# Zeros as warming weights, three rows of batch 2 transposed by DMA, and a new order of the instructions around the first two tiles

## The chip, the cores and the metric

The kernel runs on one core of one Trainium2 chip. The metric is the device time of one execution in microseconds (us). The core has five engines with queues of their own: TensorE (PE, with its weight loads shown as PEld), VectorE (DVE), ScalarE (ACT), GpSimd (POOL) and SyncE (SP). Each engine executes its instructions in program order. Transfers are issued from the queues of SP, ACT and POOL.

## The reference

Blockwise causal attention over 8 batches, 8 heads, 576 positions and head size 64, followed by a gated feed-forward layer on the result:

```python
scores = scale * np.matmul(q, k.transpose(0, 1, 3, 2))
mask = block_i >= block_j                      # blocks of 64 positions
scores = np.where(mask, scores, -1000000000.0)
attn = softmax(scores)
attn_out = np.matmul(attn, v)                  # (8, 8, 576, 64)
x = attn_out.transpose(0, 2, 1, 3).reshape(4608, 512)
gate = np.maximum(x @ w_gate, 0.0)             # 512 -> 1536
val = x @ w_val
out = (gate * val) @ w_out                     # 1536 -> 512
```

All inputs and the output are float32; the kernel computes in bfloat16 with float32 sums.

## The kernel before

**Rows.** A row `r = 4*b + hp` is one pair of heads `hp` of batch `b`; there are 32 rows. Each batch has 512 main positions (four blocks of 128) and 64 last positions, which the kernel calls tails. For a row the kernel needs q and k with the head dimension on the partitions (`qTm`, `kTm`, and `qTt`, `kTt` for the tails). Then `scores_all` makes the scores in three pieces, each in a pair of PSUM banks, and `exp` on ACT (L520) turns each piece into `attnT`; the corners of the mask are zeroed by `corners`. `head_av` (L648) multiplies with v (`v_bf`, with a column of ones for the sum) in PSUM banks 6 and 7, and `normalise` (L592 and L593 on DVE) divides and writes `xnat`. Finally `xnat` is transposed into `xT[:, hp, :]` of the batch: by `to_xT_pe` (four transposes on PE, L693, and a fifth, L699, for the 64 last positions from batch 2 on; then a copy out of PSUM by ACT or DVE), or by `to_xT_dma` (two DMA transposes on SP's queue, L707 and L711, with no work for PE). The tile `xnat` has three buffers, `xT` three.

**Feed-forward.** `ffn_gen` is a generator over nine tiles of 512 positions: tile j is batch j's main positions, tile 8 all tails. A tile has twelve groups f: four matmuls with `wg` and four with `wv` (L752), a Relu on ACT (L761), a product on DVE (L766, `hT`); then four outputs of twelve matmuls with `wo` (L782), each copied by DVE (L794, `ob`) and stored. `parts(n)` in the hand-written order emits n steps of four such matmuls, 0.86 us each; `ffn(n)` emits whole groups. They are what PE does while other engines work on the attention.

**PSUM.** `take(n)` gives the least recently taken of the banks 0 to 5 (a pair for `take(2)`). So three pairs serve the scores, the groups of the feed-forward layer and the single banks of outputs, and whoever takes a pair waits until its last user has been copied out. Banks 6 and 7 (`AV`) serve `head_av`, the transposes of batch 1 (`pe_mains`, L423) and the sorting of its v rows (`sort_v`, L373).

**Batches.** Batch 0 and 1 (class `Early`) come through staged float32 loads on SP, casts by POOL, and PE transposes. The first halves of batch 1 (heads 0 to 3: rows 4, 5) and the second (heads 4 to 7: rows 6, 7) are loaded, cast and transposed apart; `sort_v(0)` and `sort_v(4)` order the v rows of each. The tails of batches 0 and 1 are loaded together (`Tails.load`, six DMAs), cast (`cast_qk`, L213; `cast_v`, L220), transposed by eight PE transposes (`tails.pe`, L232) and copied to `qTt` and `kTt` (L240). Batch 2 and 3 are staged and cast too, but transposed by DMA (`e2.transpose`, L396, and `transpose_tails`, L438 and L439) and reordered by copies (`unpermute`, L407). From batch 4 on, POOL issues casting loads (L459), and DMA transposes write `qTm` and `kTm` directly. The stage buffers are ten, taken in turn.

**Order.** Everything is under a manual schedule: the order of the calls is the order on every engine's queue. The start has warming matmuls (`junk`, L831), which write a bank that nothing reads: the weights are `ident`, which POOL makes, the moving operand is `zeros`, which DVE sets. Then batch 0 is computed with no feed-forward work to mix in; from the first `parts(1)` on, tile 0 and then the first half of tile 1 are mixed with batch 1 by a list written out by hand (lines 902 to 1007). The loop over r = 8 to 31 does the rest in a regular way: `head_av(r-1)` around `scores_all(r)`, then the transposes of row r-1, then `ffn`. In the pass r = 8 the loads, casts and DMA transposes of batch 3 are issued; in the pass r = 11 the loads of batch 4 begin.

Of the kernel before, what the change touches and what calls it, by code (L numbers as in the profile page):

```python
# [17 lines left out]
def kernel(  # L18
# [10 lines left out]
    nc = tc.nc  # L29
# [454 lines left out]
    def load_w_half(i, g, which=(0, 1)):  # L484

        sts = []
        for t in which:
            dst, src = ((wg, moe_w_gate), (wv, moe_w_val))[t]
            lo = 512 * i + 256 * g
            st = new_stage(1024).rearrange("p (c n) -> p c n", c=4)  # L490
            nc.sync.dma_start(
                st, src[:, lo : lo + 256].rearrange("(c p) f -> p c f", p=128)
            )
            sts.append((dst[i][:, :, 256 * g : 256 * g + 256], st))
        return sts
# [4 lines left out]
    def cast_w(sts, eng):  # L500
        for dst, st in sts:
            eng(dst, st)  # L502
# [319 lines left out]
    def parts(n):  # L822

        for _ in range(n):
            next(gen)
            part[0] += 4
            done[0] += 4

    def junk(n, bank):
        for _ in range(n):  # L830
            nc.tensor.matmul(  # L831
                bank.rearrange("p (j n) -> p j n", j=4),
                ident,
                zeros[:, None, :].to_broadcast([128, 4, 128]),
                start=True,
                stop=True,
            )
# [4 lines left out]
    with tc.manual_schedule(engines={E.PE, E.DVE, E.Activation, E.Pool, E.SP}):  # L842
# [10 lines left out]
        constants(0, nc.vector)  # L853
        constants_tail(0, nc.vector)
        selection(nc.vector.memset, nc.vector.tensor_copy)
        junk(7, banks[:, 0])
        constants(1, nc.gpsimd)
        constants_tail(1, nc.gpsimd)
        token_order(pool)
# [52 lines left out]
        es = (e0, e1)  # L912
        w_2, w_out = {}, {}
        xt = sb.tile([128, 4, 128], BF, name="xtail")
        w_2[0] = load_w_half(2, 0)
        e1.load_qk(0, 4)
        parts(1)
        w_2[1] = load_w_half(2, 1)
        parts(1)
        cast_w(w_2[0], pool)  # L920
        e1.load_v_packed(0)
        e1.cast_qk(0, 4, (pool, pool))
        cast_w(w_2[1], pool)
        parts(3)
        w_out[0] = load_w_out(0)
        parts(2)
        w_out[1] = load_w_out(1)
        parts(5)
        e1.cast_v_packed(0, pool)
        parts(1)  # L930
        w_out[2] = load_w_out(2)
        parts(3)
        cast_w(w_out[0], pool)
        e1.pe_mains(0, (dve, dve), banks[:, AV : AV + 2])
        cast_w(w_out[1], pool)
        parts(1)
        e1.load_qk(4, 4)
        e1.pe_mains(1, (act, dve), banks[:, AV : AV + 2])
        cast_w(w_out[2], pool)
        scores_all(4, False)  # L940
        parts(3)
        corners(4, nc.vector)
        parts(1)
        e1.cast_qk(4, 4, (pool, pool))
        e1.sort_v(0, (act, dve), banks[:, AV : AV + 2])
        scores_all(5, False)
        heads_av(4)
        parts(1)
        e1.load_v_packed(4)
        corners(5, nc.vector)  # L950
        parts(1)
        heads_av(5)
        parts(1)
        tails.load()
        tails.cast_qk(pool)
        to_xT_pe(4, (act,), None)
        parts(3)
        e1.cast_v_packed(4, pool)
        parts(2)
        e2.load_qk(0, 4)  # L960
        e2.load_qk(4, 4)
        e2.load_v_chunks(0)
        e2.load_v_chunks(1)
        e2.load_tails((0, 1))
        e2.load_tails((2,))
        tails.cast_v(0, pool)
        e1.pe_mains(2, (dve, dve), banks[:, AV : AV + 2])
        parts(1)
        e1.pe_mains(3, (dve, dve), banks[:, AV : AV + 2])
        scores_all(6, False)  # L970
        tails.pe((dve, dve))
        corners(6, nc.vector)
        to_xT_pe(5, (act,), banks[:, AV + 1])
        scores_all(7, False)
        e1.sort_v(4, (dve, dve), banks[:, AV : AV + 2])
        parts(1)
        corners(7, nc.gpsimd)
        tails.cast_v(1, pool)
        parts(2)
        heads_av(6)  # L980
        scores_last(0)
        scores_tails(0, (0,))
        scores_tails(0, (1,))
        e2.cast_qk(0, 4, (pool, pool))
        e2.cast_qk(4, 4, (pool, pool))
        to_xT_pe(6, (act,), None)
        e2.cast_tails((pool, pool))
        heads_av(7)
        parts(1)
        e2.transpose(0)  # L990
        e2.transpose(1)
        parts(1)
        scores_last(1)
        to_xT_pe(7, (dve,), banks[:, AV + 1])
        parts(2)
        tails_av(0, 0)
        tails_av(0, 1)
        tails_of(0, xt)
        scores_tails(1, (0,))
        scores_tails(1, (1,))  # L1000
        parts(1)
        e2.unpermute(0, (dve, pool))
        parts(4)
        e2.unpermute(1, (dve, pool))
        parts(2)
        e2.transpose_tails()
        parts(1)
        for r in range(8, 4 * B):
            b, hp = divmod(r, 4)
            tails_av(1, 0) if r == 8 else head_av(r - 1, 0)  # L1010
            scores_all(r)
            tails_av(1, 1) if r == 8 else head_av(r - 1, 1)
            tails_of(1, xt) if r == 8 else heads_to_xnat(r - 1)
            if r > 12:
                to_xT_dma(r - 1)
            if r < 10:
                e2.unpermute(r - 6, (dve, dve))
            elif 11 <= r < 15:
                e3.unpermute(r - 11, (dve, dve))
            corners(r, nc.vector)  # L1020
            ffn(12 if r < 13 else 8)
            if hp == 0:
                scores_last(b)
            if 8 < r < 13:
                to_xT_pe(r - 1, (act,))
            if r == 8:
                tails_to_xT(xt, dve)
                e2.cast_v_tail(pool)
                e2.cast_v_chunks(0, pool)
                e2.cast_v_chunks(1, pool)  # L1030
                e3 = Early(3)
                e3.load_qk(0, 4)
                e3.load_tails((0, 1))
                e3.load_qk(4, 4)
                e3.load_tails((2,))
                e3.load_v_chunks(0)
                e3.load_v_chunks(1)
                e3.cast_qk(0, 4, (pool, pool))
                e3.cast_tails((pool, pool))
                e3.cast_qk(4, 4, (pool, pool))  # L1040
                e3.transpose(0)
                e3.transpose(1)
                e3.transpose_tails()
            if r == 11:
                for g in range(2):
                    e3.cast_v_chunks(g, pool)
                e3.cast_v_tail(pool)
            if hp == 3 and b + 2 < B:
                load_qkv(b + 2, (0, 1))
            if b >= 3 and b + 1 < B:  # L1050
                if hp == 0:
                    load_qkv(b + 1, (2,))
                if hp == 2:
                    dma_transposes(b + 1)
            ffn(8 if r < 12 else 0 if r == 12 else 28)
# [32 lines left out]
```

## Time and profile before

| what | value |
|---|---|
| median of 3 runs | 368.8 us (368.2 to 370.13) |
| the profiled execution, its own time | 367.89 us |
| its span, first to last instruction | 366.1 us |
| granted TensorE clock, mean | 0.999 |
| DVE, ACT, POOL busy | 46%, 46%, 31% of the span |
| moved by DMA | 51.02 MB, mean 139 GB/s |

The span lies inside the execution's own time; 1.8 us lie around it. A row of a timeline gives start, duration (of all instructions merged in the row), engine, line, operation, output and input, a count, and in brackets the idle time of the engine before it and what ended it. In the chain of waits a row has start, duration and what was on the chain then. In a table by stretches each engine has its busy time in the stretch and a count. The end of a merged PE row includes about 0.17 us in which the next matmuls already run, so PE's steps are read from start to start.

### The profile page before, as it was taken

What the parts mean: (1) busy time and instruction counts of PE and PEld (TensorE: products, weight loads), DVE (VectorE), ACT (ScalarE), POOL (GpSimd) and SP (SyncE); (2) the same over time, 40 slices, a digit from 0 to 9 for tenths busy, and PEclk for the clock granted to TensorE, in tenths of its full rate; (3) what the DMA queues carried; (4) which work ended last, traced back from release to release, by engine and by line L of the source; (5) the groups of instructions that cost most, each with busy time, mean ns of one, the idle gap of its engine ahead of it and who ended that gap; (6) DMA issues with size and microseconds to landing.
All of it is one profiled execution on the core that took longest, in us unless ns stands there. A gap on an engine that the chain in (4) does not pass through costs nothing.

```text
span 366.1 us, 7493 instructions
## 1 busy us (share of the span) xinstructions
PE 355.9 (97%) x2981; PEld 187.3 (51%) x2981; DVE 167.6 (46%) x335; ACT 167.3 (46%) x263; POOL 114.8 (31%) x158
## 2 busy tenths in 40 slices
PE   7899998999999999999999999999999999999995
PEld 3544455555555455555555555555555544444443
DVE  5744455466465543444344443544344424333432
ACT  4933716556756653565346543654264303302310
POOL 7756746275878307700590031000000000000000
PEclk9999999999999999999999999999999999999999
DMA  8999999979999979996899949173200130020013
GB/s 253 288 348 351 379 255 323 158 198 238 194 190 139 141 154 98 165 104 118 104 182 73 148 86 124 28 138 75 75 16 18 47 102 1 3 86 29 2 39 104
DMA packets 139652, 51.02 MB, mean 139 GB/s; under 512 B 117473, under 2 KB 133601, under 8 KB 139617
## 3 DMA queue, kind: packets, MB, share of 16 engines
q1 hardware_dynamic: 77952, 34.29, 41.1%
q0 software_dynamic: 56384, 7.08, 40.7%
q10 hardware_dynamic: 5280, 9.18, 7.1%
q8 instruction: 23, 0.38, 0.4%
q14 instruction: 13, 0.10, 0.1%
HBM read 37.75 MB, written 9.44 MB: 129 GB/s over the span
## 4 chain that ended last, share of the span: by engine, by line
PE 93%; ACT 4%; DVE 1%; issue 0%; POOL 0%; ACTq 0%; DVEq 0%; POOLq 0%
PE banks L752 51%; PE banks L782 25%; PE banks L648 7%; PE banks L514 6%; ACT attnT L520 2%; PE banks L831 1%; PE banks L611 1%; PE banks L693 1%; PE banks L423 1%; ACT wo L520 1%; ACT v_p L520 1%; PE banks L373 1%; DVE kTt L240 0%; DVE ob L794 0%; ACT xT L700 0%
## 5 line engine op out<-in xcount | busy, mean ns | idle before, releaser
L520 ACT ACTIVATE attnT<-banks 128x1024 bf16<-128x1024 f32 (+1 forms) x118 | 84.9, 808 | 59.7 <-PE banks L514 59.4
L761 ACT ACTIVATE gate_sb<-banks 128x512 bf16<-128x512 f32 x108 | 64.9, 603 | 102.4 <-PE banks L752 102.2
L766 DVE TENSOR_TENSOR hT<-gate_sb,banks 128x512 bf16<-128x512 bf16 x108 | 74.1, 687 | 80.5 <-PE banks L752 74.2
L752 PE MATMUL banks<-xT,wg 128*128 128x512 bf16 x384 | 99.6, 379 | 0.6 <-ACT attnT L520 0.4
L752 PE MATMUL banks<-xT,wv 128*128 128x512 bf16 x384 | 99.4, 379 | 0.0
L782 PE MATMUL banks<-wo,hT 128*128 128x512 bf16 (+1 forms) x444 | 97.2, 373 | 0.0
L752 PEld LDWEIGHTS <-wv 128*128 128x128 bf16 x432 | 42.1, 98 | 50.4 <-POOL wv L502 0.3
L782 PEld LDWEIGHTS <-hT 128*128 128x128 bf16 x444 | 42.3, 98 | 46.3 <-issue 0.2
L752 PEld LDWEIGHTS <-wg 128*128 128x128 bf16 x432 | 40.8, 98 | 46.3 <-issue 1.3
L794 DVE COPY ob<-banks 128x512 f32<-128x512 f32 (+1 forms) x37 | 25.1, 677 | 52.4 <-PE banks L782 52.3
L459 POOL DMA_DIRECT2D v_bf<-in_v_dram x16 | 14.3, 908 | 66.9 <-PE banks L648 66.9
L648 PE MATMUL banks<-v_bf,attnT 128*128 128x65 bf16 x792 | 33.4, 194 | 0.6 <-DVE attnT L579 0.3
L648 PEld LDWEIGHTS <-attnT 128*128 128x128 bf16 x792 | 29.1, 98 | 8.6 <-issue 1.0
L514 PE MATMUL banks<-qTm,kTm 64*128 64x512 bf16 (+3 forms) x256 | 25.0, 300 | 2.4 <-ACT attnT L520 1.5
L593 DVE TENSOR_TENSOR xnat<-banks,recip 128x640 bf16<-128x640 f32 (+2 forms) x36 | 25.9, 721 | 1.2
L514 PEld LDWEIGHTS <-kTm 64*128 64x128 bf16 x512 | 17.1, 94 | 10.8 <-issue 1.7
L592 DVE RECIPROCAL recip<-banks 128x10 f32<-128x10 f32 (+3 forms) x38 | 8.0, 210 | 31.2 <-PE banks L648 29.3
L459 POOL DMA_DIRECT2D k_bf<-in_k_dram x16 | 14.2, 928 | 1.7 <-DMA v_bf<-in_v_dram 1.1
L459 POOL DMA_DIRECT2D q_bf<-in_q_dram x16 | 14.4, 935 | 0.5 <-DMA v_bf<-in_v_dram 0.5
L579 DVE MEMSET attnT<- 64x192 uint32 x27 | 5.9, 218 | 18.0 <-ACT attnT L520 17.3
L752 PE MATMUL banks<-xTt,wg 128*128 128x512 bf16 x48 | 12.3, 379 | 0.0
L752 PE MATMUL banks<-xTt,wv 128*128 128x512 bf16 x48 | 12.3, 379 | 0.0
(99 smaller groups left out, 199.9 us busy)
## 6 DMA issues: line engine op xcount, KB each, us to landing
out_dram<-ob ACTq DMA_DIRECT2D x32, 256.0 KB, 2.4
stage<-in_moe_w_gate_dram SPq DMA_DIRECT2D x6, 512.0 KB, 8.7
stage<-in_moe_w_val_dram SPq DMA_DIRECT2D x6, 512.0 KB, 8.8
stage<-in_q_dram SPq DMA_DIRECT2D x6, 512.0 KB, 8.1
stage<-in_k_dram SPq DMA_DIRECT2D x6, 512.0 KB, 8.2
stage<-in_moe_w_out_dram SPq DMA_DIRECT2D x6, 512.0 KB, 9.5
stage<-in_v_dram SPq DMA_DIRECT2D x8, 256.0 KB, 6.7
q_bf<-in_q_dram POOLq DMA_DIRECT2D x16, 128.0 KB, 6.7
```

Source lines behind the costliest of these rows:

```text
L459: nc.gpsimd.dma_start(dst, src[b, :, 128 * c : 128 * c + n, :].rearrange("h p d -> p h d"),)
L514: nc.tensor.matmul(o, kTm[b % 2][ps, c, hp, :], x, start=True, stop=True)
L520: nc.scalar.activation(out, sc, AF.Exp, scale=scale)
L579: eng.memset(three[:, :, :, 0:64], 0.0)
L592: nc.vector.reciprocal(recip, av[:, :, :, 64])
L593: nc.vector.tensor_tensor(out=out, in0=av[:, :, :, 0:64], in1=recip.to_broadcast([rows, heads, n, 64]), op=AX.mult,)
L648: nc.tensor.matmul(av[:, 0, p, :], w, vb[:, c, h, :], start=(p == 0), stop=(c == p), skip_group_check=True,)
L752: nc.tensor.matmul(out[f][:, t, :], (wg, wv)[t][i][:, c, fo : fo + 128], x[:, c, :], start=(c == 0), stop=(c == 3),)
L761: nc.scalar.activation(gate[f], out[f][:, 0, :], AF.Relu)
L766: nc.vector.tensor_tensor(out=h, in0=gate[f], in1=out[f][:, 1, :], op=AX.mult)
L782: nc.tensor.matmul(ops[:, g, 0 : n1 - n0], hT[f][:, 128 * s : 128 * (s + 1)], wo[i][:, f % 4, n0:n1], start=(f == 0), stop=(f == 11),)
L794: nc.vector.tensor_copy(ob, ops[:, g, 0 : n1 - n0])
```

## The change

It has three edits. The warming matmuls take `zeros` as weights too, and the first batch of them is nine instead of seven. In the loop, rows 8, 9 and 10 (of batch 2) go to `xT` by `to_xT_dma` instead of `to_xT_pe`; row 11 stays with PE. The list of calls between the first steps of tile 0 and the loop has a new order: the loads of `w_2` and of batch 1 are written behind five steps; scores of rows 4 and 5 come before the last group of tile 0; the copies of k out of PSUM in the first two `pe_mains` go to ACT; row 5's `head_av` comes after four more output steps; the second half of batch 1 and the tails come later, with `tails.pe` behind the last output of tile 0 and `scores_all(7)` behind `sort_v(4)`; on SP the loads of the tails come before the second half of v, and the v rows of batch 2 before its q and k; on POOL `tails.cast_v(0)` comes before `tails.cast_qk`, and batch 2's casts before `tails.cast_v(1)`. The number of feed-forward steps before the loop is the same.

```diff
@@ junk @@
-                ident,
+                zeros,
                 zeros[:, None, :].to_broadcast([128, 4, 128]),
@@ start @@
-        junk(7, banks[:, 0])
+        junk(9, banks[:, 0])
@@ list @@
+        parts(5)
         w_2[0] = load_w_half(2, 0)
+        cast_w(w_2[0], pool)
         e1.load_qk(0, 4)
-        parts(1)
         w_2[1] = load_w_half(2, 1)
-        parts(1)
-        cast_w(w_2[0], pool)
+        parts(5)
+        e1.cast_qk(0, 4, (pool, pool))
         e1.load_v_packed(0)
-        e1.cast_qk(0, 4, (pool, pool))
+        parts(2)
+        w_out[0] = load_w_out(0)
+        parts(1)
         cast_w(w_2[1], pool)
+        parts(1)
+        w_out[1] = load_w_out(1)
+        parts(2)
+        e1.pe_mains(0, (dve, act), banks[:, AV : AV + 2])
+        e1.cast_v_packed(0, pool)
+        parts(1)
+        w_out[2] = load_w_out(2)
+        scores_all(4, False)
+        e1.pe_mains(1, (dve, act), banks[:, AV : AV + 2])
+        parts(2)
+        corners(4, nc.vector)
+        scores_all(5, False)
+        cast_w(w_out[0], pool)
+        cast_w(w_out[1], pool)
+        e1.load_qk(4, 4)
+        e1.sort_v(0, (act, dve), banks[:, AV : AV + 2])
+        parts(4)
+        cast_w(w_out[2], pool)
+        tails.load()
+        e1.load_v_packed(4)
+        heads_av(4)
+        corners(5, nc.vector)
+        parts(2)
+        e2.load_v_chunks(0)
+        e2.load_v_chunks(1)
         parts(3)
-        w_out[0] = load_w_out(0)
-        parts(2)
-        w_out[1] = load_w_out(1)
-        parts(5)
-        e1.cast_v_packed(0, pool)
-        parts(1)
-        w_out[2] = load_w_out(2)
-        parts(3)
-        cast_w(w_out[0], pool)
-        e1.pe_mains(0, (dve, dve), banks[:, AV : AV + 2])
-        cast_w(w_out[1], pool)
-        parts(1)
-        e1.load_qk(4, 4)
-        e1.pe_mains(1, (act, dve), banks[:, AV : AV + 2])
-        cast_w(w_out[2], pool)
-        scores_all(4, False)
-        parts(3)
-        corners(4, nc.vector)
+        heads_av(5)
         parts(1)
         e1.cast_qk(4, 4, (pool, pool))
-        e1.sort_v(0, (act, dve), banks[:, AV : AV + 2])
-        scores_all(5, False)
-        heads_av(4)
-        parts(1)
-        e1.load_v_packed(4)
-        corners(5, nc.vector)
-        parts(1)
-        heads_av(5)
-        parts(1)
-        tails.load()
-        tails.cast_qk(pool)
-        to_xT_pe(4, (act,), None)
-        parts(3)
-        e1.cast_v_packed(4, pool)
-        parts(2)
+        e1.pe_mains(2, (dve, dve), banks[:, AV : AV + 2])
+        tails.cast_v(0, pool)
+        parts(1)
+        e1.pe_mains(3, (act, dve), banks[:, AV : AV + 2])
+        scores_all(6, False)
+        to_xT_pe(4, (dve,), banks[:, AV])
+        parts(1)
         e2.load_qk(0, 4)
         e2.load_qk(4, 4)
-        e2.load_v_chunks(0)
-        e2.load_v_chunks(1)
+        to_xT_pe(5, (dve,), banks[:, AV])
         e2.load_tails((0, 1))
+        parts(1)
         e2.load_tails((2,))
-        tails.cast_v(0, pool)
-        e1.pe_mains(2, (dve, dve), banks[:, AV : AV + 2])
-        parts(1)
-        e1.pe_mains(3, (dve, dve), banks[:, AV : AV + 2])
-        scores_all(6, False)
-        tails.pe((dve, dve))
-        corners(6, nc.vector)
-        to_xT_pe(5, (act,), banks[:, AV + 1])
+        parts(1)
+        tails.cast_qk(pool)
+        tails.pe((act, dve))
+        e1.cast_v_packed(4, pool)
+        e1.sort_v(4, (dve, dve), banks[:, AV : AV + 2])
+        corners(6, nc.gpsimd)
         scores_all(7, False)
-        e1.sort_v(4, (dve, dve), banks[:, AV : AV + 2])
-        parts(1)
-        corners(7, nc.gpsimd)
-        tails.cast_v(1, pool)
-        parts(2)
         heads_av(6)
-        scores_last(0)
+        e2.cast_qk(0, 4, (pool, pool))
+        e2.cast_qk(4, 4, (pool, pool))
+        e2.cast_tails((pool, pool))
         scores_tails(0, (0,))
         scores_tails(0, (1,))
-        e2.cast_qk(0, 4, (pool, pool))
-        e2.cast_qk(4, 4, (pool, pool))
+        scores_last(0)
         to_xT_pe(6, (act,), None)
-        e2.cast_tails((pool, pool))
+        corners(7, nc.vector)
         heads_av(7)
+        parts(2)
+        to_xT_pe(7, (dve,), banks[:, AV + 1])
         parts(1)
         e2.transpose(0)
         e2.transpose(1)
-        parts(1)
-        scores_last(1)
-        to_xT_pe(7, (dve,), banks[:, AV + 1])
         parts(2)
+        tails.cast_v(1, pool)
+        parts(1)
         tails_av(0, 0)
         tails_av(0, 1)
         tails_of(0, xt)
         scores_tails(1, (0,))
         scores_tails(1, (1,))
         parts(1)
+        scores_last(1)
         e2.unpermute(0, (dve, pool))
-        parts(4)
-        e2.unpermute(1, (dve, pool))
         parts(2)
         e2.transpose_tails()
-        parts(1)
+        e2.unpermute(1, (dve, dve))
+        parts(3)
@@ loop @@
-            if r > 12:
+            if r > 8 and r != 12:
                 to_xT_dma(r - 1)
...
-            if 8 < r < 13:
+            if r == 12:
                 to_xT_pe(r - 1, (act,))
```

More of the change, by code (lines that the diff above doesn't have):

```diff
@@ L914 @@
         xt = sb.tile([128, 4, 128], BF, name="xtail")
+        parts(5)
         w_2[0] = load_w_half(2, 0)
+        cast_w(w_2[0], pool)
         e1.load_qk(0, 4)
+        w_2[1] = load_w_half(2, 1)
+        parts(5)
+        e1.cast_qk(0, 4, (pool, pool))
+        e1.load_v_packed(0)
+        parts(2)
+        w_out[0] = load_w_out(0)
         parts(1)
[L918 removed]
+        cast_w(w_2[1], pool)
         parts(1)
[L920 to L925 removed]
+        w_out[1] = load_w_out(1)
         parts(2)
[L927 to L928 removed]
+        e1.pe_mains(0, (dve, act), banks[:, AV : AV + 2])
         e1.cast_v_packed(0, pool)
```

## The prediction

> **What bounds the kernel now.** I read the page first (span, shares, chain), then the busy times by stretches, then the timelines of PE, ACT, DVE, POOL and SP where PE is not full.
>
> ```profile
> span 366.1 us, 7493 instructions
> ...
> PE 93%; ACT 4%; DVE 1%; issue 0%; POOL 0%; ACTq 0%; DVEq 0%; POOLq 0%
> ```
> ```profile
> 30.00:40.00 10.00, 9.61 (x62) 4.88 (x61) 3.84 (x7) 5.63 (x10) 6.91 (x8) 1.00 1.07 363
> 40.00:50.00 10.00, 9.59 (x99) 5.30 (x98) 4.78 (x12) 4.49 (x8) 7.05 (x8) 1.00 1.08 345
> 50.00:60.00 10.00, 8.49 (x80) 4.97 (x79) 6.70 (x17) 5.37 (x9) 4.05 (x7) 1.00 1.12 292
> 60.00:70.00 10.00, 9.66 (x177) 6.53 (x177) 4.71 (x11) 4.27 (x7) 6.52 (x11) 1.00 0.91 209
> ```
> PE carries 93% of the chain. The columns of the stretches are us, then busy time of PE, PEld, DVE, ACT and POOL, clock, DMA share, GB/s: PE misses 0.4, 0.4, 1.5 and 0.3 us of these 40, and it is here that the list is reordered. So there are three things to win: PE work itself, PE's waits between 36 and 64 us, and the start. The waits:
>
> ```profile
> 37.99 1.02 PE L752 MATMUL banks<-xT,wg 128*128 128x512 bf16 x4 [0.40 <-ACT attnT L520]
> ...
> 46.04 0.78 PE L648 MATMUL banks<-v_bf,attnT 128*128 128x65 bf16 x20 [0.29 <-DVE attnT L579]
> ...
> 55.05 0.87 PE L232 MATMUL banks<-ident,perm 128*128 128x128 bf16 x8 [0.42 <-POOL perm L213]
> 55.76 0.39 PE L693 MATMUL banks<-order,xnat 128*128 128x128 bf16 x4
> 56.46 0.97 PE L514 MATMUL banks<-qTm,kTm 64*128 64x512 bf16 x7 [0.31 <-ACT attnT L520]
> 58.00 0.27 PE L514 MATMUL banks<-qTm,kTm 64*128 64x256 bf16 x1 [0.57 <-DVE kTt L240]
> ...
> 63.47 0.40 PE L693 MATMUL banks<-order,xnat 128*128 128x128 bf16 x4 [0.34 <-DVE xnat L593]
> ```
> A row's end holds some 0.17 us of overlap, so from start to start the waits are a little longer than the brackets: 0.5 before 37.99, 0.45 before 46.04, 0.45 before 55.05, 0.5 before 56.46, 0.9 before 58.00, 0.4 before 63.47; with the small ones (0.1 to 0.25 each) about 3.9 us. No reordering can win more than that.
>
> **Edit 1, the start.**
>
> ```profile
> 0.83 0.11 DVE L108 MEMSET zeros<- 128x64 uint32 x1 [0.83 <-PEq L1072]
> 1.97 3.17 PE L831 MATMUL banks<-zeros,ident 128*128 128x512 bf16 x7 [1.97 <-POOL ident masks.py:199]
> 4.41 0.43 DVE L326 CAST q_bf<-stage 128x512 bf16<-128x512 f32 x1
> ```
> ```profile
> 5.14 0.85 PE banks L423 x8
> ...
> 35.17 0.45 PE banks L423 x8
> 35.62 0.86 PE banks L752 x4
> ```
> ```profile
> 21.76 1.04 POOL L502 CAST wv<-stage 128x1024 bf16<-128x1024 f32 x1 [0.47 <-DMA stage<-in_moe_w_val_dram]
> ...
> 22.92 1.03 PE L752 MATMUL banks<-xT,wv 128*128 128x512 bf16 x4
> ```
> Eight transposes take 0.85 us at 5.14 and 0.45 at 35.17: PE runs at half speed at first, although the clock column reads 1.00. Today the warming waits for POOL's `ident` until 1.97; with zeros alone it waits for DVE only (0.83 + 0.11) and starts near 1.0. Nine matmuls of 3.17/7 = 0.45 end by 5.0, about when the first cast (4.41 + 0.43 = 4.84) lets the transposes begin: no delay, 0.1 at worst. If full speed comes 1 us sooner, the first transposes and scores win up to 0.6 us. But the win ends at 22.92: that step needs `wv`, cast at 21.76 + 1.04 = 22.80 after a wait for DMA, and the loads do not move. So 0.12 us can pass. I take -0.1, with ends of +0.1 and -0.12. The Trainium skill (TensorE: Matmul & The Clock Gate, on the clock gate) says that warm-up is a free-running window of about 3.4 us and not a count of matmuls; by it the two extra matmuls bring nothing, and the earlier start brings between nothing and a whole window, by the window's phase: in the first case this edit is worth 0 and the sum below is 366.7. Half speed still at 5.14, 3.2 us after the first matmul, agrees with a window; the phase no row here shows.
>
> **Edit 2, the order.** Up to 35.17 PE's sequence is unchanged, and the loads and casts that it needs keep their order on SP and POOL. From there I walk through the new list, each engine in the order of its queue, with these durations:
>
> ```profile
> 36.59 0.69 DVE L766 TENSOR_TENSOR hT<-gate_sb,banks 128x512 bf16<-128x512 bf16 x1 [0.40 <-PE banks L752]
> ...
> 56.22 1.73 DVE L240 COPY kTt<-banks 64x256 bf16<-64x256 bf16 x4
> ...
> 59.09 1.29 DVE L382 CAST v_bf<-banks 128x512 bf16<-128x512 f32 x2 [0.86 <-PE banks L373]
> ```
> ```profile
> 36.74 0.58 ACT L435 COPY qTm<-banks 128x512 bf16<-128x512 bf16 x1 [0.94 <-PE banks L423]
> 37.34 2.49 ACT L520 ACTIVATE attnT<-banks 128x512 bf16<-128x512 f32 x4
> 39.69 0.63 ACT L761 ACTIVATE gate_sb<-banks 128x512 bf16<-128x512 f32 x1
> ```
> ```profile
> 58.27 0.87 PE banks L373 x16
> ```
> First half, rows 4 and 5. The k copy on ACT (0.58, behind a Relu) lets the scores of row 4 start at 36.4; their last piece takes the pair of group 9 and waits for its product (36.59 + 0.69 = 37.28). Group 10 waits for the first exps until 38.0, as today. Then ACT has in its queue four exps (2.49, from 36.9 to 39.4), the next k copy (to 39.9) and only then group 10's Relu (to 40.5), and DVE its product (to 41.2). Row 5's scores, now ahead of the last group, wait 0.2 for that k copy, and their last piece, which takes group 10's pair, 0.8 for that product. With the sorting (0.87) and group 11 (two steps of 0.86, the row at 35.62) the outputs start at 44.0, and after two steps and row 4's attention PE stands at 46.3, where it stood at 45.6 before. Of these 0.7 us, 0.45 come back: row 5's exps are long done, so the wait before 46.04 is gone. About +0.3 at 52 us.
>
> Second half, rows 6, 7 and tails. POOL's casts for rows 6 and 7 wait for loads that don't move; the six tail DMAs go ahead of the second half of v on SP, so the tails' casts are done some 2 us before `tails.pe`, now at 57.9: the waits before 55.05, 55.76 and 56.46 go. What comes instead: 0.1 to 0.3 for row 4's transposes behind the q copy on ACT, as much for the next output behind row 6's first exp; 0.75 for the last piece of row 7's scores, which takes the pair of `tails.pe` and waits for the four kTt copies (1.73, from 58.7 to 60.4); 1.0 for row 6's attention, because the two sorting copies (1.29) queue on DVE behind those and now no output step covers them; 0.5 for `xnat` of row 6. That is 2.7 us of waits where 3.3 stood, with row 7's attention ending at 64.2:
>
> ```profile
> 63.87 0.61 PE banks L648 x20
> ```
> Before it ended at 63.87 + 0.61 = 64.48, with the same work done. So edit 2 is worth -0.3; its ends are -3.3 (only row 6's `xnat` and a bank are still waited for) and +3.2 (below). Behind 64 us it is SP's queue that moves:
>
> ```profile
> SPq L289 <- POOL q_bf L315: 3.9, 2, 2.5
> ```
> Today the four loads of batch 2's v rows (L289) stand behind its q and k and wait 3.9 us for POOL's casts. They now go ahead of q and k, at a time when nothing holds them; q and k come later, but everything behind them on SP, batch 2's transposes and batch 3's loads and transposes, starts sooner by part of that 3.9: I estimate 2.5 us.
>
> **Edit 3, three rows by DMA.**
>
> ```profile
> 88.66 0.22 PE banks L693 x4
> 88.89 0.06 PE banks L699
> ```
> ```profile
> 98.84 1.27 SPq L439 DMA_TRANSPOSE kTt<-k_bt  x1
> ```
> ```profile
> kTt<-k_bt SPq DMA_TRANSPOSE x1, 7.4
> ```
> ```profile
> xT<-xnat SPq DMA_TRANSPOSE x20, 2.6
> ```
> ```profile
> 106.59 0.82 DVE L593 TENSOR_TENSOR xnat<-banks,recip 128x640 bf16<-128x640 f32 x1
> ```
> ```profile
> 108.83 0.39 PE L693 MATMUL banks<-ident,xnat 128*128 128x128 bf16 x4
> ...
> 110.90 1.03 PE L752 MATMUL banks<-xT,wg 128*128 128x512 bf16 x4
> ```
> PE loses 3 x (0.22 + 0.06) = 0.84 us of work on a stretch where it never waits: -0.85. SP gains six transposes, about 1.25 us each like the one shown, behind batch 3's, whose last issue ends at 98.84 + 1.27 = 100.1 today and 2.5 sooner, at 97.5, by the estimate above. Two things wait for them: row 11's `xnat` (106.59, or 105.7 with three rows saved) reuses row 8's buffer, and tile 2 (110.90, then 110.0) reads rows 8 to 10. A landing takes 2.6 in the median, but 7.4 at this place. From 97.5, row 8's second one is issued at 98.7 and lands near 106.2: DVE waits 0.5, which PE does not feel, since it takes `xnat` only at 108.83 - 0.85. Row 10's lands near 110, just in time. So -0.85, with +1.1 as the other end (below).
>
> **Sum.** 367.89 (the profiled execution) - 0.1 - 0.3 - 0.85 = 366.6. That execution lies 0.9 under the median of the runs, 368.8; on the median the forecast is 368.8 - 1.25 = 367.5. A measurement of this kernel can tell about 0.5%, or 1.84 us, from no change.
>
> **Rivals.**
> - *The second half's waits vanish too.* If the kTt and sorting copies finish before PE asks (they need about 1 us), edit 2 gives -2 to -3.3: 364.5 to 366. For it: all inputs are there 1 to 2 us early. Against: both stand in one queue on DVE, and the outputs that could cover them are used up.
> - *The second half of v comes late* (slower). Its load now stands behind the six tail DMAs:
>
> ```profile
> stage<-in_v_dram SPq DMA_DIRECT2D x2, 512.0 KB, 10.3
> ```
> ```profile
> 46.67 1.84 SPq L204 DMA_DIRECT2D stage<-in_v_dram  x2
> ```
> It takes the place at which the tails' last issue ends today, 46.67 + 1.84 = 48.5. Issued at 49 and landing after 10.3 us, cast in 1.04 (the `wv` row's length), it lets `sort_v(4)` start at 60.3, not 58.3. Of the delay 1.0 hides in the waits already counted, the rest is paid in full, with no output step left as cover. It decides from a landing after 58.3; at a landing of 61.4 it costs 3.2: 368.8 - 1.25 + 3.2 = 370.7 or more.
> - *The DMA transposes land late.* If SP is free only at 100.1, row 8 lands at 101.3 + 7.4 = 108.7, row 11's `xnat` ends at 109.5 and PE waits 1.5; row 10 lands at 112.6 and costs 0.4 more. 367.5 + 1.95 = 369.5. It decides from SP being free after 98.5. The Trainium skill (DMA: Bandwidth & Descriptors, Rules for kernel authors) speaks for it: all queues' transfers interleave on the same 16 engines; 7.4 against 2.6, with POOL's loads of batch 4 in flight, agrees.
> - *Zeros don't warm.* Half speed would last some 3 us more, at most +1: 367.5 to 368.5. Against: the moving operand is zeros already.
>
> **Chances.** Forecast 0.45 (its own range 366.2 to 368.4, of which 0.18 lies under 366.96), first rival 0.24, late v 0.14 (0.12 over 370.64), late transposes 0.12 (0.04 over, if each lands still later), no warming 0.05. Faster by over 0.5%: 0.18 + 0.24 = 0.42; slower: 0.12 + 0.04 = 0.16; within: 0.42. The range from 364.9 to 370.5 leaves out the ends of the first two rivals.
>
> **What would show it.** Right: the first L831 at 1.0; L752 with `wv` still behind its cast near 22.8; row 7's attention ending near 64.2, with waits on kTt (L240) and on v_bf (L382) near 60 to 62; no L693 for rows 8 to 10; tile 2 starting near 110 without a wait. Wrong: a wait of PE on POOL's v_p cast near 58 to 62, waits on `xnat` or on xT near 108 to 113, or no waits at all around 60.

## The result, and the profile after

| | median, us | lowest to highest | ratio to before, 95% interval |
|---|---|---|---|
| before | 368.98 | 368.2 to 370.13 (6) | |
| after | 374.53 | 373.31 to 375.04 (6) | 1.0143 [1.0118, 1.0167] |

The change costs 5.55 us of the median. The profiled execution of the kernel after took 375.04 us, the longest of its six, and that of before 367.89 us, less than any of the six in the table; so the two profiles lie 7.15 us apart. First the head of the page of after, to be read against 366.1 us and the chain of before, where PE had 93%:

```profile
span 373.3 us, 7473 instructions
...
PE 87%; DMA 7%; DVE 2%; ACT 1%; SPq 1%; POOL 1%; issue 0%; ACTq 0%; POOLq 0%
```

PE's share of the chain is down, and there is a new entry, DMA 7%. Some two thirds of it are loads before 23 us, where the chain of before runs through PE and ACT to nearly the same step (22.92 and 23.07); 10.35 us are one piece that before did not have. The chain in order of time (start, us, what) around it:

```profile
100.08 10.35 DMA xT<-xnat
...
110.51 0.34 ACTq L720
...
110.95 0.60 ACT attnT L520
111.56 0.04 issue
111.60 4.30 PE banks L782 x12
```

Row 8's DMA transpose lands 10.35 us after its issue, and *then ACT issues a store of the output* (L720). Behind the store stand row 12's exps (L520), and PE's next matmuls wait for those exps: they need a PSUM bank that an exp has to read first. The timelines of ACT, PE and DVE after show the same (start, duration, instruction, idle time before it and what ended it):

```profile
110.95 0.60 ACT L520 ACTIVATE attnT<-banks 128x512 bf16<-128x512 f32 x1 [8.76 <-DMA xT<-xnat]
```
```profile
111.60 4.30 PE L782 MATMUL banks<-wo,hT 128*128 128x512 bf16 x12 [4.44 <-ACT attnT L520]
```
```profile
111.31 0.82 DVE L593 TENSOR_TENSOR xnat<-banks,recip 128x640 bf16<-128x640 f32 x1 [3.88 <-DMA xTt<-xnat]
```

Before, these 12 matmuls stood at 106.12 with no wait, took 2.75, and DVE's L593 came at 106.59:

```profile
106.12 2.75 PE L782 MATMUL banks<-wo,hT 128*128 128x512 bf16 x12
```

Two holds are thus in one place: ACT for row 8's xT, DVE for row 8's xTt. Why does a store wait for a transpose? A completion semaphore is the counter that a transfer raises when it has landed. In the order of the built program, transfers of SP and ACT take eight completion semaphores in turn, and a transfer waits until the last user of its semaphore has landed. From that listing (not from the trace; queue, number in it, line, kind, output and input, shape, what it waits for):

```
SP   84 L707 DmaTransposeAnt xT_1407<-xnat_1403 128x4x128 [waits DMAHW7_49,DVE_49]
SP   85 L711 DmaTransposeAnt xTt_95<-xnat_1403 128x1x64 [waits DMAHW0_49]
ACT  84 L720 DMACopy out_0_dram<-ob_1595 128x512 [waits DMAHW7_49,DVE_49]
ACT  88 L720 DMACopy out_0_dram<-ob_1628 128x512 [waits DMAHW0_49]
```

The two stores come eight transfers behind row 8's two, on the same semaphores: they are issued at 110.51 and 111.26, just after row 8's two have landed at 100.08 + 10.35 = 110.43 and 101.85 + 9.4 = 111.25. So the trace bears the listing out.

The stretches of the kernel after (us; busy PE, PEld, DVE, ACT, POOL; granted clock, DMA share, GB/s):

```profile
60.00:64.00 4.00, 2.56 (x66) 1.78 (x63) 3.12 (x7) 3.24 (x5) 1.04 (x1) 0.95 0.98 320
64.00:68.00 4.00, 4.00 (x35) 2.46 (x34) 1.08 (x4) 1.95 (x4) 2.08 (x2) 0.63 1.22 294
...
108.00:112.00 4.00, 0.40 (x2) 0.12 (x2) 0.69 (x1) 1.05 (x3) 2.64 (x3) 0.92 2.75 128
112.00:116.00 4.00, 4.00 (x19) 1.70 (x18) 1.51 (x6) 1.87 (x3) 1.51 (x2) 0.65 1.78 123
```

PE does nothing from 107.2 to 111.6, and the clock it is granted then falls: 0.65 in the mean of the next stretch, 0.50 from 112 to 114, and the 12 matmuls take 4.30 instead of 2.75. A second fall, to 0.63, comes at 64 to 68, behind a stretch in which PE was busy 2.56 of 4 us in small waits.

The account starts at the last tail matmul (L611), before, after, and in `all_late2`, an experiment below with the same order and no fall of the clock there:

```profile
79.41 0.20 PE L611 MATMUL banks<-v_bf,attnD 128*128 128x65 bf16 x1
81.32 0.20 PE L611 MATMUL banks<-v_bf,attnD 128*128 128x65 bf16 x1
79.90 0.20 PE L611 MATMUL banks<-v_bf,attnD 128*128 128x65 bf16 x1
```

It starts 1.9 us later, 1.4 of it by that fall of the clock. The wait gives +4.4, the half clock behind it +1.5, the saved transposes some -0.9; together 6.9, and row 11's attention is 7.0 later (116.13 against 109.11). From there both kernels go on at one pace.

### The profile page after: what moved, and what is told of

Read it like the earlier page. It is cut to its first block, busy times and chain, and to the rows that moved or that the text cites. A ratio compares the mean times of both kernels' runs of the same rounds, so it can differ in the third digit from the quotient of the medians.

```text
span 373.3 us, 7473 instructions
## 1 busy us (share of the span) xinstructions
PE 359.0 (96%) x2968; PEld 187.6 (50%) x2968; DVE 168.2 (45%) x334; ACT 165.7 (44%) x259; POOL 113.8 (30%) x157
## 4 chain that ended last, share of the span: by engine, by line
PE 87%; DMA 7%; DVE 2%; ACT 1%; SPq 1%; POOL 1%; issue 0%; ACTq 0%; POOLq 0%
PE banks L752 49%; PE banks L782 24%; PE banks L648 7%; PE banks L514 5%; DMA xT<-xnat 3%; DMA stage<-in_moe_w_val_dram 2%; DMA stage<-in_v_dram 1%; DMA stage<-in_k_dram 1%; PE banks L611 1%; SPq L279 1%; ACT attnT L520 1%; DVE kTt L240 0%; PE banks L693 0%; PE banks L423 0%; DVE xnat L593 0%
## 5 line engine op out<-in xcount | busy, mean ns | idle before, releaser
L520 ACT ACTIVATE attnT<-banks 128x1024 bf16<-128x1024 f32 (+1 forms) x118 | 84.9, 806 | 63.7 <-PE banks L514 49.1
L782 PE MATMUL banks<-wo,hT 128*128 128x512 bf16 (+1 forms) x444 | 98.7, 377 | 4.5 <-ACT attnT L520 4.4
L752 PE MATMUL banks<-xT,wg 128*128 128x512 bf16 x384 | 99.9, 380 | 0.7 <-ACT xT L700 0.7
L752 PE MATMUL banks<-xT,wv 128*128 128x512 bf16 x384 | 99.8, 380 | 0.1
L782 PEld LDWEIGHTS <-hT 128*128 128x128 bf16 x444 | 42.9, 99 | 52.1 <-issue 6.6
L752 PEld LDWEIGHTS <-wv 128*128 128x128 bf16 x432 | 42.1, 98 | 50.9 <-POOL wv L502 0.6
L752 PEld LDWEIGHTS <-wg 128*128 128x128 bf16 x432 | 40.7, 98 | 46.5 <-issue 0.9
L648 PEld LDWEIGHTS <-attnT 128*128 128x128 bf16 x792 | 29.9, 98 | 10.1 <-issue 2.1
L593 DVE TENSOR_TENSOR xnat<-banks,recip 128x640 bf16<-128x640 f32 (+2 forms) x36 | 26.0, 721 | 5.1 <-DMA xTt<-xnat 3.9
L752 PE MATMUL banks<-xTt,wg 128*128 128x512 bf16 x48 | 12.3, 379 | 0.0
L752 PE MATMUL banks<-xTt,wv 128*128 128x512 bf16 x48 | 12.3, 379 | 0.0
```

The source lines that it names most:

```text
L520: nc.scalar.activation(out, sc, AF.Exp, scale=scale)
L593: nc.vector.tensor_tensor(out=out, in0=av[:, :, :, 0:64], in1=recip.to_broadcast([rows, heads, n, 64]), op=AX.mult,)
L648: nc.tensor.matmul(av[:, 0, p, :], w, vb[:, c, h, :], start=(p == 0), stop=(c == p), skip_group_check=True,)
L752: nc.tensor.matmul(out[f][:, t, :], (wg, wv)[t][i][:, c, fo : fo + 128], x[:, c, :], start=(c == 0), stop=(c == 3),)
L782: nc.tensor.matmul(ops[:, g, 0 : n1 - n0], hT[f][:, 128 * s : 128 * (s + 1)], wo[i][:, f % 4, n0:n1], start=(f == 0), stop=(f == 11),)
```

## The experiments

Each was timed in turn with the kernel before on one chip; ratios are to that.

**1. Which edit.** Four kernels. `zeros_only`: the kernel before with only the first edit (zeros as both operands, 9 instead of 7). `zeros_order`: the kernel after with the old rows (`if r > 12: to_xT_dma(r - 1)`, `if 8 < r < 13: to_xT_pe(r - 1, (act,))`). `rows_only` and `rows_8_9`: the kernel before with

```
rows_only                            rows_8_9
-            if r > 12:               -            if r > 12:
+            if r > 8 and r != 12:    +            if r in (9, 10) or r > 12:
                 to_xT_dma(r - 1)                      to_xT_dma(r - 1)
...
-            if 8 < r < 13:           -            if 8 < r < 13:
+            if r == 12:              +            if r in (11, 12):
                 to_xT_pe(r - 1, (act,))               to_xT_pe(r - 1, (act,))
```

> The kernel before with the first edit alone (zeros as weights, nine warming matmuls). Main theory (the loss comes from the three rows and from the new order, the start gives nothing because the weights' loads set the pace until 23 us): the first warming matmul at 1.0, the first exp near 6.7 instead of 7.4, tile 0 no earlier than before, time 0.998 to 1.002 of the kernel before. Rival (the earlier start passes through): 0.998 or less, some 0.7 us.

> The changed kernel with rows 8 to 10 transposed by PE again (edits one and two, not three). Main theory: the list costs some 1.5 to 2 us, nearly all of it because the clock falls to half near 64 us for about 3 us; granted clock 0.995; 370.5 to 371.0. Rival A (the fall is an accident of the profiled execution): 368.4 to 369.2. Rival B (the new order of SP's and POOL's queues is what makes the DMA of the rows late, and it costs in other places too): over 372.

> The kernel before with the third edit alone. Main theory (row 8's transposes land 8 to 10 us after issue; stores on ACT's queue, whose turn of completion semaphores comes back to row 8's transposes, hold ACT; PE waits 4 us and then runs at half speed for some 3 us): 372.5 to 374, ACT idle some 8 us near 100 to 110, granted clock 0.995. Rival (late only behind the new order): 368.1 to 368.5.

> The kernel before with rows 8 and 9 alone by DMA (rows 10 and 11 by PE). Two transfers fewer stand between row 8's transposes and the stores, so the store that waited for row 8 now waits for one that is two earlier. If ACT's queue, held by that store, is the cause: no wait of ACT on xT, at most 1.5 us of wait on batch 3's last transpose; what is left is row 11's xnat behind row 8's landing: 368 to 370.5. If the late landing itself is the cause, through the reuse of xnat and the reading of xT: 371 or more, with PE's wait in front of L693 or of tile 2.

| | median, us | ratio, 95% |
|---|---|---|
| before | 368.19 | |
| zeros_only | 367.95 | 0.9984 [0.9961, 1.0007] |
| zeros_order | 367.93 | 0.9985 [0.9965, 1.0005] |
| rows_only | 374.96 | 1.0174 [1.0125, 1.0222] |
| rows_8_9 | 372.19 | 1.0106 [1.0052, 1.016] |

The rows are the whole loss; `rows_only` lies 1.0 us over the expected 374. The theory that the new order itself costs time by a fallen clock near 64 us was wrong, and `zeros_order` lies under its rival A too (368.4): it makes the same walk with the same waits, and its clock stays up:

```profile
60.00:64.00 4.00, 2.82 (x78) 2.24 (x78) 2.63 (x7) 3.36 (x6) 1.28 (x2) 1.00 1.04 335
64.00:68.00 4.00, 3.95 (x30) 2.00 (x28) 1.37 (x4) 1.94 (x5) 1.84 (x2) 1.00 1.46 270
```

With two rows only, no store of this stretch has row 8's semaphore, ACT's stores go at 103.86 and 108.23, and still there is a hole, as the second branch of the expectation has it (371 or more). The timelines of PE and DVE in `rows_8_9`:

```profile
113.75 0.61 PE L693 MATMUL banks<-ident,xnat 128*128 128x128 bf16 x4 [4.01 <-DVE xnat L593]
```
```profile
112.87 0.82 DVE L593 TENSOR_TENSOR xnat<-banks,recip 128x640 bf16<-128x640 f32 x1 [5.57 <-DMA xTt<-xnat]
```

This is the buffer: `xnat` has three, and row 11's is row 8's, which the transposes have not read yet. That profiled execution (376.25 us) also has a granted clock of 0.50 from 58 to 60 us, with the *old* order: so part of its 4 us over the median has another cause than the rows.

**2. The two holds apart, and the landing.** All four build on `rows_only`.

```
rows_sp_store:   (nc.sync if j == 1 else nc.scalar).dma_start(out[r0 : r0 + 128, :], ob)
rows_xnat5:      if r in (11, 12): xnats[r] = (five blocks in a free stage buffer)
rows_both:       both
rows_late_loads:
-            if hp == 3 and b + 2 < B:
+            if hp == 3 and b + 2 < B and b != 2:
                 load_qkv(b + 2, (0, 1))
             if b >= 3 and b + 1 < B:
                 if hp == 0:
                     load_qkv(b + 1, (2,))
+                    if b == 3:
+                        load_qkv(4, (0, 1))
```

> The kernel before with rows 8 to 10 by DMA, and tile 1's four stores issued on SP's queue instead of ACT's. In the kernel with the rows by DMA alone ACT stands from 100.2 to 109 us behind a store that waits for row 8's transpose, and DVE's normalisation of row 11 stands until 111.7 for row 8's xTt, whose source is its buffer (three of them). Theory (two holds, one behind the other): with the store gone row 12's exps come near 101 to 106 us, PE goes through its 12 output matmuls without the wait of 4.5 us, and then stops for xnat of row 11, which still waits for row 8's landing near 111 us; 371 to 372.5 us, as with rows 8 and 9 alone. Rival (ACT's store is the whole loss): 367.5 to 369 us. Rival (the store has nothing to do with it): 375 us with the exps still near 109.

> The kernel before with rows 8 to 10 by DMA, and rows 11 and 12 given buffers of their own for xnat, so that row 11's normalisation no longer waits for row 8's transposes to have read theirs. Theory (two holds): the normalisation of row 11 comes near 105.7 instead of 111.7, but PE's wait of 4.5 us for row 12's exps stays, since ACT still stands behind the store until row 8 has landed near 109: 373.5 to 375 us. Rival (the buffer is the whole loss): 367.5 to 369 us.

> Both edits: tile 1's stores on SP's queue, and buffers of their own for xnat of rows 11 and 12. Theory: neither hold is left, PE reaches tile 2's first matmul near 110.5 us, and only the rows themselves can be late: row 10's transposes are issued at 107 to 108 and land 8 us later, so tile 2's third and fourth pieces wait to 115 or 116 us, 3 to 5 us, of which the outputs' order lets nothing be filled: 370 to 373 us. Rival (the two holds are all the loss, the rows are in time): 367 to 368.5 us.

> The kernel before with rows 8 to 10 by DMA, and POOL's casting loads of batch 4's q and k moved behind its loads of v, which wait for a tile of v to be read near 106 us: so no casting load is in flight when row 8's and row 9's transposes are issued. Theory (the loads in flight make the transposes late): row 8 lands in 2.5 to 4 us as the rows do where no such load runs, row 9 in under 6, ACT's store and DVE's xnat wait for nothing, and at most row 10 is late, by 3 us: 367.3 to 370 us. Rival (the transposes stand behind one another on SP's queue, whatever else runs): landing 8 to 10 us as before, 374 to 375 us.

| | median, us | ratio, 95% | xT landing (median, rows 8 to 10) |
|---|---|---|---|
| before | 367.99 | | |
| rows_sp_store | 373.06 | 1.0143 [1.0086, 1.02] | 8.8 |
| rows_xnat5 | 374.57 | 1.0174 [1.0143, 1.0204] | 8.0 |
| rows_both | 370.85 | 1.0084 [1.0051, 1.0117] | 7.8 |
| rows_late_loads | 370.11 | 1.0073 [1.0039, 1.0107] | 3.4 |

`rows_xnat5` and `rows_both` lie in the expected ranges; `rows_sp_store` lies 0.6 us over the expected 372.5 (its profiled execution took 371.05), `rows_late_loads` 0.1 over the expected 370. Against `rows_only` (374.96, timed with another run of before), taking away the store's hold alone gives 1.9 us and the buffer's alone 0.4, since the other stands beside it; taking both away gives 4.1, and what is left is what PE itself reads late. PE's timelines in `rows_sp_store`, `rows_xnat5` and `rows_both` (in the last two, four lines were added, so L786 is L782 and L756 is L752):

```profile
110.19 0.40 PE L693 MATMUL banks<-ident,xnat 128*128 128x128 bf16 x4 [2.22 <-DVE xnat L593]
111.77 0.60 PE L648 MATMUL banks<-v_bf,attnT 128*128 128x65 bf16 x14 [1.13 <-DVE attnT L579]
```
```profile
106.95 0.29 PE L514 MATMUL banks<-qTt,kTm 64*128 64x64 bf16 x8 [2.38 <-DMA qTt<-q_bt]
...
111.05 4.96 PE L786 MATMUL banks<-wo,hT 128*128 128x512 bf16 x12 [3.25 <-ACT attnT L520]
```
```profile
105.46 0.29 PE L514 MATMUL banks<-qTt,kTm 64*128 64x64 bf16 x8 [0.73 <-DMA qTt<-q_bt]
...
112.36 0.38 PE L756 MATMUL banks<-xT,wg 128*128 128x512 bf16 x1 [1.01 <-DMA xT<-xnat]
113.63 0.59 PE L756 MATMUL banks<-xT,wg 128*128 128x512 bf16 x2 [0.89 <-DMA xT<-xnat]
```

So the late landing is felt in four places, one behind the other: batch 3's own `qTt`, ACT's store, DVE's buffer, tile 2's reads. The wait for `qTt` was not expected, and stands in these two profiles only. That transpose is issued ahead of the rows' on SP and landed in 9.7 and 9.0 us (6.0 before, 6.5 in `rows_only`); why it was later there is not shown. So the time of `rows_xnat5` agrees with the theory partly by luck: its profile has 3.25 us of wait for ACT instead of the expected 4.5, and 2.38 for `qTt`. With all of this cured at the root, by loads that start at 105.45 instead of near 96, row 8's transposes stand alone. The DMA queues between 98 and 105.4 us in `rows_late_loads` (where q0, POOL's casting loads, has no line at all) and between 100 and 109 in the kernel after:

```profile
q1 hardware_dynamic: 2110, 0.49, 33.3%
...
xT<-xnat SPq DMA_TRANSPOSE x3, 3.4
```
```profile
q0 software_dynamic: 4527, 0.57, 134.2%
...
xT<-xnat SPq DMA_TRANSPOSE x3, 9.7
```

Six transposes stand one behind another on SP in both; only the loads differ. Rows 8 to 10 land in 2.9, 3.4 and 4.8 us, the last beside batch 4's loads of v. The rival that the queue itself makes them late is out; whether the casting matters, or any load of this size would do, was not tried. PE in `rows_late_loads` waits for nothing there and reaches tile 2 at 109.87, 1.03 us ahead of before (110.90). But this comes back as a wait 28 us later, 0.70 in the fastest of its executions, because batch 4's `kTm` now lands in 10.8 us beside batch 5's loads (6.0 before). That execution is the profiled one, 368.10 us; where the median's other 2 us go was not profiled.

```profile
109.87 1.03 PE L752 MATMUL banks<-xT,wg 128*128 128x512 bf16 x4
...
138.46 0.72 PE L514 MATMUL banks<-qTm,kTm 64*128 64x512 bf16 x8 [0.70 <-DMA kTm<-k_bf]
```

**3. The loads of both batches moved.** In three kernels the condition is `b not in (2, 3)` and the moved call stands under `if b in (3, 4): load_qkv(b + 1, (0, 1))`: on the kernel before (`late2_only`), on `rows_only` (`rows_late2`) and on the kernel after (`all_late2`).

> The kernel before with one edit, no row by DMA: POOL's casting loads of q and k of batches 4 and 5 are moved behind the loads of v of the same batch, each by one row. The loads are off PE's path and are needed by the transposes of q and k near 123 and 160 us. Theory (a load moved back costs nothing as long as it lands ahead of those transposes, and with batch 5's moved too the stretch from 121 to 137 us is free of casting loads): 367.5 to 368.5 us, no change. Rival (the loads need all the time from 95 us): kTm of batch 4 late near 138 us, 368.5 to 370.5 us.

> The kernel with rows 8 to 10 by DMA and batch 4's loads late reached tile 2 at 109.87 us where the kernel before reached it at 110.90, and lost this again near 138 us, where kTm of batch 4 landed 0.7 us late (in the fastest of its executions) beside batch 5's casting loads. Here batch 5's loads are moved back as well. Theory (the rows by DMA do bring the PE time that they save, once no casting load is in flight beside a transpose that PE waits for): tile 2 at 109.9, no wait near 138, 366.8 to 367.8 us. Rival (the casting loads have to run beside something, and the wait only moves on): 368.5 to 370.5 us.

> The kernel after the change with the same move of the casting loads of batches 4 and 5: all three edits, without the collision. Theory: tile 2 near 109.5 us, 366.5 to 367.8 us, the forecast's sign and about its size. Rival as in the run with the rows alone: 368.5 to 370.5 us.

| | median, us | lowest to highest | ratio, 95% |
|---|---|---|---|
| before | 368.07 | 367.64 to 371.27 | |
| late2_only | 367.96 | 367.36 to 368.25 | 0.9978 [0.9956, 0.9999] |
| rows_late2 | 369.35 | 367.83 to 374.23 | 1.0032 [1.0007, 1.0057] |
| all_late2 | 367.62 | 366.98 to 373.15 | 0.9984 [0.9969, 0.9999] |

The move alone costs nothing, as expected. `rows_late2` came out as its rival had it: no wait is left near 138, but the wait moved on, to row 10, which is issued at 105.87 as batch 4's loads of v begin (105.14). PE's timeline:

```profile
112.48 0.38 PE L752 MATMUL banks<-xT,wg 128*128 128x512 bf16 x1 [2.32 <-DMA xT<-xnat]
```

`all_late2` has no such wait in its profile (the loads of v begin at 106.41 there, behind row 10's issue at 105.93, which landed in 4.1 us instead of 6.6) and takes back the whole loss: 6.9 us below the kernel after, though measured beside another run of before. Its interval ends just under 1, but so does that of `late2_only`, which has none of the three edits; a gain from them is not shown. Tile 2 starts at 110.83, not near 109.5 as expected.

**4. What the rows are worth.** `order_late2` is `zeros_order` with the same move; `all_late2_8_9` is `all_late2` with row 10 back on PE (conditions as in `rows_8_9`).

> Zeros, the new order and the casting loads of batches 4 and 5 moved back, with no row by DMA: beside the run of all three edits with the same move (367.62 us) it shows what the rows by DMA are worth when nothing collides. Theory (the saved PE time counts where no row is late): this kernel is slower than that one by 0.3 to 0.8 us, 367.8 to 368.2 us. Rival (the rows by DMA bring nothing even then): 367.4 to 367.7 us.

> All three edits with the move, but row 10 transposed by PE again: row 10's transposes are issued near 106 us, when batch 4's loads of v begin, and landed 6.6 us later in the run of the rows with both batches' loads late, where PE waited 2.32 us for them. Theory: rows 8 and 9 land before those loads, PE waits for no row in any execution, one row's saving of 0.28 us is given up: 367.2 to 367.9 us, and no execution 3 us above the others. Rival (row 10 was not what made executions slow): the spread of 367 to 373 us stays.

| | median, us | lowest to highest | ratio, 95% |
|---|---|---|---|
| before | 367.98 | 367.4 to 371.52 | |
| order_late2 | 367.89 | 367.68 to 369.81 | 0.9997 [0.9979, 1.0014] |
| all_late2_8_9 | 367.90 | 367.38 to 369.37 | 0.9986 [0.9965, 1.0008] |

With row 10 on PE no execution lies 3 us above the others; that fits the lateness of row 10 in `rows_late2`, but the one of 373.15 was not profiled. The theory wanted 0.3 to 0.8 us between `order_late2` and `all_late2`: the medians differ by 0.27, the intervals overlap. That the rows save PE time is shown with the old order (1.03 us at tile 2 in `rows_late_loads`); that they save time at the end is not. With the new order tile 2 starts at 110.83 in `all_late2` and at 110.84 in `order_late2`. Counted from the step with `wv` that the prediction shows at 22.92 (23.03 and 22.52 in these two), the saving is 0.5 us; most of the rest goes near 91 us, where the scores of one row take 1.14 us in `all_late2` instead of 0.78, and the profile shows no wait for it.

The same order drops its clock in one profile and not in another, at the same busy share of PE; `all_late2_8_9`, then `all_late2`:

```profile
60.00:64.00 4.00, 2.55 (x66) 1.77 (x63) 3.12 (x7) 3.21 (x5) 1.08 (x2) 0.96 1.02 345
64.00:68.00 4.00, 3.78 (x32) 2.42 (x32) 1.10 (x4) 1.97 (x4) 2.81 (x3) 0.61 1.28 280
```
```profile
60.00:64.00 4.00, 2.55 (x68) 1.79 (x62) 3.12 (x7) 3.28 (x5) 1.04 (x1) 1.00 1.03 314
64.00:68.00 4.00, 3.95 (x42) 2.26 (x41) 1.46 (x5) 1.94 (x5) 2.09 (x2) 1.00 1.22 272
```

## Why the prediction was wrong

The forecast was 367.5 us; 374.53 lies above the range. By its steps:

**Edit 1: right.** The step said that full speed comes sooner and that the gain is swallowed by the DMA-bound `wv`. PE's timeline after, at the start, and later at that step:

```profile
1.00 4.02 PE L831 MATMUL banks<-zeros 128*128 128x512 bf16 x9 [1.00 <-DVE zeros L108]
4.88 0.61 PE L423 MATMUL banks<-ident,q_bf 128*128 128x128 bf16 x4
5.28 0.51 PE L423 MATMUL banks<-ident,k_bf 128*128 128x128 bf16 x4
5.63 0.59 PE L831 MATMUL banks<-zeros 128*128 128x512 bf16 x2
...
23.07 1.04 PE L752 MATMUL banks<-xT,wv 128*128 128x512 bf16 x4
```

The warming starts at 1.00, full speed comes during the transposes at 5.28 (before, the four at 5.36 still took 0.63), scores start at 6.27 instead of 6.78, and `wv`'s step stands at 23.07 behind a cast that ended at 23.01: nothing is left. The same step comes at 22.40 in `rows_only`, with the old start, and in `zeros_order`, with the new one: the loads decide. Forecast -0.1; `zeros_only` gives 0.9984 [0.9961, 1.0007]. Zeros do warm: that rival is out. When full speed comes differs between profiles of the same start, by over 2 us for the old one (near 5.0 in `rows_late2`, near 7.2 in `late2_only`) and over 1 us for the new (4.4 in `all_late2`, 5.6 in `zeros_only`). This agrees with the free-running window of the Trainium skill (TensorE: Matmul & The Clock Gate, on the clock gate) that the prediction cited.

**Edit 2: right in its waits, wrong in its size and in what follows on SP.** The waits that were to take the place of the old ones are there, with the engine and line named; PE's timeline after:

```profile
44.11 1.89 PE L782 MATMUL banks<-wo,hT 128*128 128x512 bf16 x8
...
60.88 0.27 PE L514 MATMUL banks<-qTm,kTm 64*128 64x256 bf16 x1 [0.46 <-DVE kTt L240]
61.60 0.31 PE L648 MATMUL banks<-v_bf,attnT 128*128 128x65 bf16 x5 [0.46 <-DVE v_bf L382]
62.20 0.61 PE L648 MATMUL banks<-v_bf,attnT 128*128 128x65 bf16 x15 [0.29 <-DVE v_bf L382]
...
63.84 0.61 PE L693 MATMUL banks<-order,xnat 128*128 128x128 bf16 x4 [0.23 <-DVE xnat L593]
64.24 1.31 PE L648 MATMUL banks<-v_bf,attnT 128*128 128x65 bf16 x20
```

Outputs at 44.11 (forecast 44.0), row 7's attention from 64.24 to 65.55 in this execution at half clock (forecast end 64.2); in `zeros_order` it runs from 63.48 to 64.26. That this is the forecast end is luck, since its `wv` step came at 22.40, 0.5 us ahead of before's 22.92. From that step to the last L611 the old order takes 56.5 us in before and in five other profiles, and up to 56.87, in `rows_only`, which starts as early as `zeros_order`; the new order takes 56.87 in all three profiles without a fall of the clock:

```profile
63.48 0.78 PE L648 MATMUL banks<-v_bf,attnT 128*128 128x65 bf16 x20
...
79.27 0.20 PE L611 MATMUL banks<-v_bf,attnD 128*128 128x65 bf16 x1
```

So on before's start the edit costs 0.4 us where -0.3 was forecast, and on an early start nothing. One slip lies in the sum: of its 3.9 us of old waits, 0.5 and 0.45 stand before 52 us, which leaves at most 2.95 for the second half and not the 3.3 that it set against 2.7. Where the rest goes was not traced. The end does not show it: `zeros_order` against `zeros_only` is 367.93 to 367.95. The rivals of the vanished waits and of the late second half of v did not come. The fall of the clock was not in the prediction; it cost this execution about 1.4 us (81.32 against 79.90 for the same matmul in `all_late2`), but it is not the price of the order, which ran without it in three other profiles.

**The step between, "2.5 us sooner" on SP: wrong.** Batch 2's first transpose is indeed issued 2.6 us sooner, at 65.33, but that issue lasts 3.77 us (1.34 before), its second follows only at 69.21, and by batch 3's last the gain is gone. SP's timeline after:

```profile
65.33 3.77 SPq L396 DMA_TRANSPOSE perm<-q_bf  x1
69.21 1.24 SPq L396 DMA_TRANSPOSE perm<-k_bf  x1
...
98.06 1.94 SPq L439 DMA_TRANSPOSE kTt<-k_bt  x1
100.08 1.71 SPq L707 DMA_TRANSPOSE xT<-xnat  x1
101.85 2.59 SPq L711 DMA_TRANSPOSE xTt<-xnat  x1
```

SP was free at 100.0, not at 97.5. That is the condition of the third rival ("decides from SP being free after 98.5"), which was given 0.12 and 369.5 us. But SP's time is not what decides: in `rows_late_loads` SP is free at 99.0, and no row is late.

**Edit 3: the step that failed.** Its PE saving was right (-0.85 forecast, -1.03 seen at tile 2 in `rows_late_loads`). Its waits were mis-sized and its list of waiters was short. Landing was taken as 7.4, the worst transpose of before in that place; the six new ones took 10.4 to 8.2, beside the casting loads (xT 3.4 in the median without those). "Two things wait for them", the prediction said, row 11's `xnat` and tile 2. A third does: ACT's queue, through a store that shares a completion semaphore in turn. The issue of a DMA was costed on its own queue, not on the queue that comes eight transfers later. And what follows a hole of 4.4 us, half a clock for the next 12 matmuls, was in no sum. So instead of -0.85, or +1.1 at the other end, the edit costs 6.8 us (374.96 against 368.19). The third rival had the right event, for the loads in flight that it names, with a condition that does not decide and less than a third of the price.

## What to carry to other kernels

Moving small work from a full engine to DMA is worth its time only where the transfers land as fast as the median row says: look which queues are in flight at that place, and price the landing there, with the new transfers added. List everything that waits for such a transfer: its readers, the next user of its source buffer, and the transfers on other queues that take its completion semaphore in turn, with what stands behind those. Even with every landing in time, the PE work saved here did not show at the end. A hold that has a second one beside it shows little when taken away alone; take them away together, or cure the cause.

## What was not expected of the hardware

- The DMA transposes `xT` of rows 8 and 9 landed in 2.9 and 3.4 us with no casting load in flight; the medians were 7.8 to 9.7 beside the loads of q and k, and row 10's landed in 4.1 to 6.6 where only loads of v were beside it. It is the same for the larger ones: batch 4's `kTm` landed in 4.8 to 6.6 us where batch 5's loads were moved away, in 10.8 beside them.
- After 4.4 us with PE idle the granted clock was 0.65 in the mean of the next 4 us. It also fell, to 0.61 and 0.63, behind a stretch in which PE was busy 2.55 of 4 us and no single wait was over 0.5 us, and did not fall in three other kernels with the same walk (2.55, 2.68 and 2.82 of 4). What decides this was not tried and stays open.
